# When the next weight piece is prepared, and two fill calls of one group, in a fused retention and two-MLP kernel

## Chip, cores and metric

One core of a Trainium2 chip runs the whole program. The metric is device time in microseconds (us), the median of several executions. TensorE (PE) multiplies, VectorE (DVE) and ScalarE (ACT) work element by element, GpSimd (POOL) helps at the start, SyncE's queue (SP) starts most DMAs. Each engine runs its own queue in the order in which the program issued it, so an instruction that waits holds up all that is behind it on that engine.

## What is computed

A retention layer (2 x 8 heads, 768 tokens, 64 channels, float32), whose output is laid out as 1536 tokens of 512 channels, and two MLPs behind it:

```python
    h = x @ w_in                                        # first MLP, 512 -> 2048
    g = np.maximum(h, 0.0) + alpha * np.minimum(h, 0.0)
    x = (g @ w_out).astype(np.float32)                  # 2048 -> 512
    h = x @ w_in2                                       # second MLP
    r = np.maximum(h, 0.0)
    return ((r * r) @ w_out2).astype(np.float32)
```

## The kernel before

**Numbers.** A float32 operand of a matmul is split into a high part (rounded, type float32r) and a low part (the rest), and each product of two operands is three matmuls: low by high, high by low, high by high. The split of an operand is a copy to the high part on ScalarE and a subtraction on VectorE.

**Stages.** The retention runs to about 53 us, the first MLP to about 309 us (its matmuls are L235 and L281; the last blocks of L281 run between those of the second MLP's first group), the second MLP to the end (L490 and L574).

**The second MLP** runs 16 groups n = 0 to 15, each one half u of the tokens (768 of them) with one pair p of the 16 slices of the hidden layer. The two halves of a group's hidden values come from seven products P0 to P6 (Strassen's scheme, six matmuls of 384 columns each, L490), into two PSUM banks px and py, with copies and sums between them. Behind them come the output matmuls of the group before, in six items of six matmuls of 512 columns (L574); group 0 has the last eight L281 items of three matmuls there. `strassen` writes the order of a group by hand:

- P0 into px, then ScalarE's copy of px to py (L515), and the split of the second half of the group before (L507, L508)
- fill 0; two output items; P1 into py, copy u2 on ScalarE (L523); P2 into px; relu and square of one quarter (ScalarE L502, VectorE L503)
- fill 1; one item; P3 into py, copy u3 on ScalarE (L531)
- fill 2; one item; P4 into a new px, VectorE's sum of px and u3 (L538)
- fill 3; P5 into py, relu and square (L502, L503), split of the first half (L507, L508); one item; P6 into px, VectorE's L547 and L550
- fill 4; one item

P1 waits for L515, P3 for L523, P5 for L531, P6 for L538, P0 of the next group for the L503 behind P5. In group 0 a last L281 item ends a sum on VectorE (L302) and writes it out on SP's queue (L308).

**The fills.** `fill(us)` takes steps from the generators in the list `fillers`, the first one first, until the costs that they yield use up its budget; a call with budget 0 takes none. Two generators stand there. `convert_pairs` turns the weights of the second MLP into high and low parts, 16 pieces k (two slices each, even k for the first matrix, odd k for the second; an even piece also gets four sums for Strassen's scheme). `split_x` prepares the seven token operands of a half; while it has steps it stands first. The steps of piece k, with their costs, are:

- shift (VectorE L372, cost 0.7), sign (VectorE L374, 1.2)
- the two low parts of piece k-1 (VectorE L360, 1.2 each for an even piece, 0.7 each for an odd one); then the buffer of k-1's bits is free
- start of piece k+1 (ScalarE L344 and L345, in the buffer that k-1 had, from the raw words of k+1) and, in the same step, the add of piece k (VectorE L381, 1.2)
- the raw words of k are free, the loads of piece k+2 go on SP's queue (L332, two of 512 KB); for an even piece two sums (L389, L390, cost 0.8), then two more (L392, L393, 0.8)
- two copies to the high part (ScalarE L399), in one step with the shift of piece k+1

The copies wait until the places of the weights in SBUF are free (pieces from 8 on reuse places of earlier pairs); till then a fill passes to nothing. `need` forces steps when a group asks for a weight that isn't there yet. The fills also run twice in each of the last 16 steps of the first MLP, with a budget of 1.2.

Of the kernel before, what the change touches and what calls it, by code (L numbers as in the profile page):

```python
# [41 lines left out]
BLOCKS = 2 * HALF // CH  # L42
GROUPS = [(0, p) for p in range(4)] + [(1, p) for p in range(NPF)] + [(0, p) for p in range(4, NPF)]
FILL = 1.2, 2.0, 1.2, 0.7, 1.5
KB = 256
ORDER = [(n // B, n % B) for n in range(NN)]

# [16 lines left out]
class Block:  # L64
# [8 lines left out]
    def free(self):  # L73
        n = self.words // KB
        self.units[self.at : self.at + n] = [True] * n


class Memory:
# [3 lines left out]
    def add(self, ap):  # L82
        self.spans.append((ap, [True] * (ap.shape[1] // KB)))

# [32 lines left out]
def retention_then_two_mlps(  # L117
# [100 lines left out]
    def release(blocks):  # L218
        for block in blocks:
            block.free()  # L220
# [102 lines left out]
    def convert_pairs():  # L323

        raw, bit, done = {}, {}, {}

        def load(k):
            if k < len(pieces):
                half, p = pieces[k]
                raw[k] = yield from taken(LOW, RAW + 8 * (k % 2), 8)  # L330
                for e in range(2):
                    nc.sync.dma_start(  # L332
                        raw[k].view(U32)[:, 2 * e * DM : 2 * (e + 1) * DM],
                        w2[2 * (2 * p + e) + half],
                    )

        def start(k):
            if k < len(pieces):
                half, p = pieces[k]
                bit[k] = yield from taken(LOW, BIT + 7 * half, 4 if half else 7)  # L340
                both = raw[k].view(U32, 2)
                low, high = both[:, :, 0], both[:, :, 1]
                x = bit[k].view(F32)[:, 0 : 2 * DM]
                nc.scalar.activation(x, high.bitcast(F32), AF.Copy, scale=REBIAS)  # L344
                nc.scalar.activation(low.bitcast(I32), low, AF.Copy, scale=2.0**-29)  # L345

        def cuts(k):
            half, p = pieces[k]
            x, b = bit[k].view(F32), done[k]
            if half:  # L350
                for e in range(2):
                    yield x[:, e * DM : (e + 1) * DM], b[e].ap, b[2 + e].ap
            else:
                for c in slice(0, 2 * DM), slice(2 * DM, None):
                    yield x[:, c], b[0].ap[:, c], b[1].ap[:, c]

        def lows(k):
            if k >= 0:
                for x, hi, lo in cuts(k):
                    nc.vector.tensor_tensor(lo, x, hi.bitcast(F32), ALU.subtract)  # L360
                    yield 0.7 if pieces[k][0] else 1.2
                bit.pop(k).free()
                pairs[pieces[k]] = done.pop(k)

        yield from load(0)
        yield from load(1)
        yield 0
        yield from start(0)
        for k, (half, p) in enumerate(pieces):
            both = raw[k].view(U32, 2)  # L370
            x = bit[k].view(U32)[:, 0 : 2 * DM]
            nc.vector.tensor_scalar(x, x, 3, None, ALU.logical_shift_left)  # L372
            yield 0.7
            nc.vector.scalar_tensor_tensor(  # L374
                x, both[:, :, 1], 0x80000000, x, ALU.bitwise_and, ALU.bitwise_or
            )
            yield 1.2
            yield from lows(k - 1)
            yield from start(k + 1)
            x = x.bitcast(I32)  # L380
            nc.vector.tensor_tensor(x, x, both[:, :, 0].bitcast(I32), ALU.add)  # L381
            yield 1.2
            raw.pop(k).free()
            yield from load(k + 2)
            if half == 0:
                a11, a12, a21, a22, s1, s2, s4 = (
                    bit[k].view(F32)[:, i * DM // 2 : (i + 1) * DM // 2] for i in range(7)
                )
                nc.vector.tensor_tensor(s1, a21, a22, ALU.add)  # L389
                nc.vector.tensor_tensor(s2, s1, a11, ALU.subtract)  # L390
                yield 0.8
                nc.vector.tensor_tensor(a21, a11, a21, ALU.subtract)  # L392
                nc.vector.tensor_tensor(s4, a12, s2, ALU.subtract)  # L393
                yield 0.8
            done[k] = []
            for span, at in PAIRS_AT[p % 4][2] if half else PAIRS_AT[p % 4][0:2]:
                done[k].append((yield from taken(span, at, 2 if half else 7)))
            for x, hi, lo in cuts(k):
                nc.scalar.copy(hi, x)  # L399
        yield from lows(len(pieces) - 1)  # L400
# [52 lines left out]
    def fill(us):  # L453
        for gen in list(fillers):
            while us > 0:
                cost = next(gen, "end")
                if cost == "end":
                    fillers.remove(gen)
                if cost is None or cost == "end":
                    break  # L460
                us -= cost

    def need(table, key, gen):
        while key not in table:
            cost = next(gen)
            assert cost is not None, (key, "no room")
        return table[key]

    makers = {}
# [8 lines left out]
    def strassen(n, items):  # L478

        u, p = GROUPS[n]  # L480
        v = sum(b <= n for b in begins) - 1
        banks = (n % 2,), (1 - n % 2,)
        def product(ps, i, start=False):
            name, a = WANTED[i]
            xh, xl = (x.view(F32R, HALF) for x in need(x_parts, (v, name), makers["x", v]))
            wh, wl = (w.view(F32R) for w in need(pairs, (0, p), makers["w"]))
            for c in range(2):
                cols = slice((2 * a + c) * 128, (2 * a + c + 1) * 128)
                for j, (w, x) in enumerate(((wl, xh), (wh, xl), (wh, xh))):
                    nc.tensor.matmul(  # L490
                        ps, w[:, cols], x[:, c, :], start=start and c == 0 and j == 0,
                        stop=c == 1 and j == 2, skip_group_check=True,
                    )
            if n in ends:
                release(x_parts.pop((v, name)))

        def other(count=1):
            for item in islice(items, count):
                item()

        def relu_square(out, ps):
            nc.scalar.activation(out, ps, AF.Relu)  # L502
            nc.vector.scalar_tensor_tensor(out, ps, 0.0, out, ALU.max, ALU.mult)  # L503

        def halves(block):
            hi, lo = borrow(F32R), borrow(F32R)
            nc.scalar.copy(hi.view(F32R), block.view(F32))  # L507
            nc.vector.tensor_tensor(lo.view(F32R), block.view(F32), hi.view(F32), ALU.subtract)  # L508
            spare[F32].append(block)
            return hi, lo  # L510

        px = bank(f"p1_{n}", banks[0])[:, 0:HALF]
        product(px, 0, True)
        py = bank(f"p6_{n}", banks[1])[:, 0:HALF]
        nc.scalar.copy(py, px)  # L515
        if n > 0:
            pending.pop()()
        fill(FILL[0])
        other(2 if n > 0 else 4)
        product(py, 1)  # L520
        us = borrow()
        u2, u3 = (us.view(F32, HALF)[:, i] for i in range(2))
        nc.scalar.copy(u2, py)  # L523
        product(px, 2)
        first_half = borrow()
        g = first_half.view(F32, HALF)
        relu_square(g[:, 0], px)
        fill(FILL[1])
        other(1 if n > 0 else 2)
        product(py, 3)  # L530
        nc.scalar.copy(u3, py)  # L531
        fill(FILL[2])
        other()
        px = bank(f"p5_{n}", banks[0])[:, 0:HALF]
        product(px, 4, True)
        second_half = borrow()
        h = second_half.view(F32, HALF)
        nc.vector.tensor_tensor(h[:, 1], px, u3, ALU.add)  # L538
        fill(FILL[3])
        product(py, 5)  # L540
        relu_square(g[:, 1], py)
        ga = halves(first_half)
        other()
        product(px, 6)
        if n == visits[p][-1]:
            release(pairs.pop((0, p)))
        nc.vector.tensor_tensor(h[:, 0], px, u2, ALU.add)  # L547
        spare[F32].append(us)
        h = second_half.view(F32)
        nc.vector.scalar_tensor_tensor(h, h, 0.0, h, ALU.max, ALU.mult)  # L550
        gs = [ga, None]

        def late():
            gs[1] = halves(second_half)

        pending.append(late)
        fill(FILL[4])
        other()
        return gs

# [436 lines left out]
```

## Time and profile before

| what | value |
|---|---|
| median of 3 runs | 579.86 us (577.70 to 580.03) |
| the profiled execution's own time | 579.38 us |
| its span, first to last instruction | 577.3 us |
| TensorE busy | 565.1 us, 98% |
| VectorE busy | 379.3 us, 66% |
| ScalarE busy | 309.6 us, 54% |
| share of TensorE in the chain that ended last | 85% |

A stretch of a timeline row is its start, its length, engine and line, and in brackets how long the engine had been idle and what ended that. The end of a matmul is modelled, so a row's start is compared with the start of a later row.

### The profile page before, as it was taken

How to read it: one execution, taken by the hardware profiler on the slowest of the kernel's cores; microseconds unless marked ns; L12 is line 12 of the kernel's file. 1: busy time of each engine (PE TensorE's matmuls, PEld its weight loads, DVE VectorE, ACT ScalarE, POOL GpSimd, SP SyncE). 2: the span in 40 equal slices, each digit the busy share in tenths (PEclk: the TensorE clock that was granted, in tenths of full speed). 3: DMA queues.
4: the chain of work that ended last, by engine and by line, in shares of the span. 5: the costliest groups of instructions: out<-in, count | busy, mean ns of one | idle time of the engine just before them, and what ended most of it. 6: DMA issues, size and time to landing. Idle time of an engine off the chain costs nothing.

```text
span 577.3 us, 8029 instructions
## 1 busy us (share of the span) xinstructions
PE 565.1 (98%) x3154; PEld 485.5 (84%) x3154; DVE 379.3 (66%) x552; ACT 309.6 (54%) x506; POOL 33.9 (6%) x34
## 2 busy tenths in 40 slices
PE   8999999999999999999999799999999999999997
PEld 8887888888888888888888599899888988898985
DVE  3897866666666667887575786656777783752235
ACT  2666775765746766666465453465455543452221
POOL 2784000000000000000000000000000000000000
PEclk9999999999999999999999989999999999999999
DMA  7992343323533252434800535012013500023002
GB/s 261 383 391 102 110 145 110 128 91 110 196 132 110 80 196 89 165 127 146 307 22 0 179 115 182 0 74 99 32 59 140 182 1 1 0 93 127 1 0 109
DMA packets 30148, 69.20 MB, mean 120 GB/s; under 512 B 3224, under 2 KB 7328, under 8 KB 30112
## 3 DMA queue, kind: packets, MB, share of 16 engines
q1 hardware_dynamic: 26512, 55.60, 26.9%
q10 hardware_dynamic: 3600, 13.11, 6.7%
q8 instruction: 24, 0.39, 0.3%
q14 instruction: 12, 0.10, 0.1%
HBM read 56.63 MB, written 12.07 MB: 119 GB/s over the span
## 4 chain that ended last, share of the span: by engine, by line
PE 85%; DVE 5%; ACT 4%; DMA 4%; issue 1%; SPq 0%; ACTq 0%; DVEq 0%
PE h L235 23%; PE acc L281 22%; PE acc L574 19%; PE p L490 16%; PE o L771 2%; PE o L779 2%; PE s L734 1%; DMA q<-in_qt_dram 1%; ACT low_mem L344 1%; ACT low_mem L345 1%; PE pk L794 1%; DMA r<-in_kr_dram 1%; DMA zd<-z 1%; DMA low_mem<-in_w_dram 1%; DVE low_r_mem L360 1%
## 5 line engine op out<-in xcount | busy, mean ns | idle before, releaser
L574 PE MATMUL acc<-high_r_mem,low_r_mem 128*128 128x512 f32 x288 | 73.4, 396 | 0.2
L574 PE MATMUL acc<-low_r_mem 128*128 128x512 f32 x288 | 73.0, 393 | 0.0
L281 PE MATMUL acc<-low_r_mem,high_r_mem 128*128 128x512 f32 x288 | 69.6, 389 | 0.0
L281 PE MATMUL acc<-low_r_mem 128*128 128x512 f32 x288 | 69.4, 389 | 0.0
L235 PE MATMUL h<-low_r_mem,high_r_mem 128*128 128x512 f32 x288 | 69.2, 389 | 0.0
L235 PE MATMUL h<-low_r_mem 128*128 128x512 f32 x288 | 69.0, 390 | 0.0
L252 DVE SCALAR_TENSOR_TENSOR high_mem<-h,high_mem 128x512 f32<-128x512 f32 x44 | 30.4, 690 | 52.4 <-ACT high_mem L251 52.3
L281 PEld LDWEIGHTS acc<-low_r_mem 128*128 128x128 f32 x288 | 54.0, 188 | 11.5 <-DVE high_mem L302 0.3
L235 PEld LDWEIGHTS h<-low_r_mem 128*128 128x128 f32 x288 | 54.0, 188 | 11.4 <-issue 0.2
L235 PEld LDWEIGHTS h<-low_r_mem,high_r_mem 128*128 128x128 f32 x288 | 54.0, 188 | 11.2
L281 PEld LDWEIGHTS acc<-low_r_mem,high_r_mem 128*128 128x128 f32 x288 | 54.0, 188 | 11.0
L574 PEld LDWEIGHTS acc<-high_r_mem,low_r_mem 128*128 128x128 f32 x288 | 54.1, 190 | 10.3 <-DVE low_r_mem L508 1.0
L574 PEld LDWEIGHTS acc<-low_r_mem 128*128 128x128 f32 x288 | 53.4, 188 | 9.0
L490 PE MATMUL p<-low_r_mem 128*128 128x384 f32 x288 | 57.0, 341 | 2.9 <-ACT p L515 2.7
L490 PEld LDWEIGHTS p<-low_r_mem 128*128 128x128 f32 x288 | 51.7, 190 | 6.7 <-ACT p L515 3.1
L257 ACT CAST low_r_mem<-high_mem 128x512 fp32r<-128x512 f32 x48 | 29.8, 621 | 51.0 <-DVE high_mem L252 37.8
L490 PE MATMUL p<-low_r_mem,high_r_mem 128*128 128x384 f32 x288 | 55.5, 336 | 0.3 <-DVE high_mem L503 0.3
L490 PEld LDWEIGHTS p<-low_r_mem,high_r_mem 128*128 128x128 f32 x288 | 51.1, 188 | 3.4 <-DVE high_mem L503 0.7
L508 DVE TENSOR_TENSOR low_r_mem<-high_mem,low_r_mem 128x768 fp32r<-128x768 f32 x32 | 30.6, 956 | 27.8 <-ACT low_r_mem L507 27.8
L262 DVE TENSOR_TENSOR low_r_mem<-high_mem,low_r_mem 128x512 fp32r<-128x512 f32 x48 | 33.2, 692 | 16.2 <-ACT low_r_mem L257 13.7
L503 DVE SCALAR_TENSOR_TENSOR high_mem<-p,high_mem 128x384 f32<-128x384 f32 x32 | 17.8, 556 | 38.7 <-ACT high_mem L502 38.7
L250 ACT ACTIVATE high_mem<-h 128x512 f32<-128x512 f32 x44 | 26.2, 596 | 31.7 <-PE h L235 31.7
(97 smaller groups left out, 726.9 us busy)
## 6 DMA issues: line engine op xcount, KB each, us to landing
low_mem<-in_w_dram SPq DMA_DIRECT2D x39, 512.0 KB, 4.1
low_mem<-in_w_dram ACTq DMA_DIRECT2D x25, 512.0 KB, 3.3
sums<-high_mem SPq DMA_DIRECT2D x22, 256.0 KB, 2.2
high_mem<-xs SPq DMA_DIRECT2D x12, 384.0 KB, 5.7
high_mem<-sums SPq DMA_DIRECT2D x16, 256.0 KB, 5.5
k<-in_kt_dram SPq DMA_DIRECT2D x12, 256.0 KB, 5.8
q<-in_qt_dram SPq DMA_DIRECT2D x12, 256.0 KB, 5.0
v<-in_vr_dram SPq DMA_DIRECT2D x12, 256.0 KB, 5.8
```

Source lines behind the costliest of these rows:

```text
L235: nc.tensor.matmul(ph, w[:, cols], x[:, c, :], start=c == 0 and i == 0, stop=c == NC - 1 and i == 2)
L250: nc.scalar.activation(g, ph, AF.Relu, scale=-1.0)
L252: nc.vector.scalar_tensor_tensor(g, ph, 0.0, g, ALU.max, ALU.subtract)
L257: nc.scalar.copy(gh.view(F32R)[:, 0:TT], g)
L262: nc.vector.tensor_tensor(gl.view(F32R)[:, 0:TT], g.view(F32)[:, 0:TT], gh.view(F32)[:, 0:TT], ALU.subtract)
L281: nc.tensor.matmul(acc[t][i], w[:, cols], g, start=f == part[0] and j == 0, stop=f == part[-1] and j == 2,)
L490: nc.tensor.matmul(ps, w[:, cols], x[:, c, :], start=start and c == 0 and j == 0, stop=c == 1 and j == 2, skip_group_check=True,)
L503: nc.vector.scalar_tensor_tensor(out, ps, 0.0, out, ALU.max, ALU.mult)
L508: nc.vector.tensor_tensor(lo.view(F32R), block.view(F32), hi.view(F32), ALU.subtract)
L574: nc.tensor.matmul(acc2[j], g[:, e, rows], w, start=n in begins and e == 0 and i == 0, stop=n in ends and e == 1 and i == 2,)
L771: nc.tensor.matmul(po[t * D : (t + 1) * D, a, :], v_t[:, 2 * a + t, :], sc[:, t, a, :], start=a == 0, stop=c == 0, skip_group_check=True,)
L779: nc.tensor.matmul(po[d, a, :], state[b, c % 2][d, a, :], q_t[d, a, :], start=False, stop=True, skip_group_check=True,)
```

## The change

In `convert_pairs` the start of piece k+1 moves from ahead of the add of piece k to behind it. The add yields 1.2, so the start now belongs to the next step: that with the loads of piece k+2 and, for an even piece, the first two sums, or, for an odd one, the copies and the next shift. The costs stay. The budgets of group 0 become `FILL_0`, with 0 in place of 1.2 and 0.7 for fills 2 and 3. `need` takes the end of a generator without an exception, as long as the weight is there by then.

```diff
 FILL = 1.2, 2.0, 1.2, 0.7, 1.5
+FILL_0 = 1.2, 2.0, 0.0, 0.0, 1.5
...
             yield 1.2
             yield from lows(k - 1)
-            yield from start(k + 1)
             x = x.bitcast(I32)
             nc.vector.tensor_tensor(x, x, both[:, :, 0].bitcast(I32), ALU.add)
             yield 1.2
+            yield from start(k + 1)
             raw.pop(k).free()
             yield from load(k + 2)
...
         while key not in table:
-            cost = next(gen)
+            cost = next(gen, "end")
             assert cost is not None, (key, "no room")
+            assert cost != "end" or key in table
...
+        budget = FILL if n > 0 else FILL_0
...
-        fill(FILL[0])
+        fill(budget[0])
...
-        fill(FILL[1])
+        fill(budget[1])
...
-        fill(FILL[2])
+        fill(budget[2])
...
-        fill(FILL[3])
+        fill(budget[3])
...
-        fill(FILL[4])
+        fill(budget[4])
```

## Rows read from the trace of the kernel before

**Rows 1.** The page: TensorE's busy time; granted clock of forty slices, in tenths.

```profile
PE 565.1 (98%) x3154; PEld 485.5 (84%) x3154; DVE 379.3 (66%) x552; ACT 309.6 (54%) x506; POOL 33.9 (6%) x34
...
PEclk9999999999999999999999989999999999999999
```

**Rows 2.** TensorE's waits: line and releaser, us in total, times, longest.

```profile
PE p L490 <- ACT p L515: 2.7, 1, 2.7
...
PE p L490 <- DVE high_mem L538: 1.4, 1, 1.4
```

**Rows 3.** Timeline of TensorE, second MLP: start, length, engine, line, count.

```profile
313.17 2.27 PE L490 MATMUL p<-low_r_mem,high_r_mem 128*128 128x384 f32 x12
...
320.51 0.86 PE L281 MATMUL acc<-low_r_mem,high_r_mem 128*128 128x512 f32 x3
...
330.92 3.28 PE L490 MATMUL p<-low_r_mem 128*128 128x384 f32 x12 [2.69 <-ACT p L515]
...
345.48 2.92 PE L574 MATMUL acc<-low_r_mem 128*128 128x512 f32 x12
...
348.24 2.27 PE L490 MATMUL p<-low_r_mem 128*128 128x384 f32 x12
...
363.88 2.27 PE L490 MATMUL p<-low_r_mem,high_r_mem 128*128 128x384 f32 x12
...
410.87 2.27 PE L490 MATMUL p<-low_r_mem 128*128 128x384 f32 x12
...
426.96 2.27 PE L490 MATMUL p<-low_r_mem,high_r_mem 128*128 128x384 f32 x12
...
443.47 2.27 PE L490 MATMUL p<-low_r_mem,high_r_mem 128*128 128x384 f32 x12
...
459.11 2.27 PE L490 MATMUL p<-low_r_mem 128*128 128x384 f32 x12
...
475.10 2.27 PE L490 MATMUL p<-low_r_mem 128*128 128x384 f32 x12
```

**Rows 4.** Timeline of VectorE and ScalarE, groups 0 and 1.

```profile
318.47 1.28 DVE L302 TENSOR_TENSOR high_mem<-acc,high_mem 128x512 f32<-128x512 f32 x2
...
318.59 1.14 ACT L399 CAST low_r_mem<-low_mem 128x512 fp32r<-128x512 f32 x2 [0.18 <-DVE low_mem L381]
...
319.67 0.68 DVE L372 TENSOR_SCALAR low_mem<-low_mem 128x1024 uint32<-128x1024 uint32 x1
...
320.38 1.23 DVE L374 SCALAR_TENSOR_TENSOR low_mem<-low_mem 128x1024 uint32<-128x1024 uint32 x1
...
322.13 0.55 DVE L538 TENSOR_TENSOR high_mem<-p,high_mem 128x384 f32<-128x384 f32 x1
...
323.77 0.84 ACT L507 CAST low_r_mem<-high_mem 128x768 fp32r<-128x768 f32 x1 [2.58 <-DVE high_mem L503]
...
328.35 1.15 ACT L344 ACTIVATE low_mem<-low_mem 128x1024 f32<-128x1024 f32 x1 [3.73 <-DVE low_r_mem L360]
...
330.38 0.49 ACT L515 COPY p<-p 128x384 f32<-128x384 f32 x1
```

**Rows 5.** Windows: stretch, us, busy PE, PEld, DVE, ACT, POOL, PEclk, DMA, GB/s.

```profile
332.10:335.50 3.40, 3.40 (x11) 3.11 (x11) 2.69 (x7) 1.75 (x3) 0.00 (x0) 0.50 0.41 157
...
330.92:348.24 17.32, 17.32 (x78) 15.62 (x79) 14.20 (x20) 9.59 (x14) 0.00 (x0) 0.90 0.45 154
...
348.24:363.88 15.64, 15.64 (x79) 14.08 (x78) 9.04 (x15) 6.69 (x10) 0.00 (x0) 1.00 0.34 127
```

**Rows 6.** Timeline of ScalarE, groups 6 and 7.

```profile
415.54 1.19 ACT L344 ACTIVATE low_mem<-low_mem 128x1024 f32<-128x1024 f32 x1 [1.87 <-DVE high_r_mem L360]
...
436.06 1.13 ACT L344 ACTIVATE low_mem<-low_mem 128x1024 f32<-128x1024 f32 x1 [2.83 <-DMA low_mem<-in_w_dram]
```

**Rows 7.** DMA issues from 300 to 350: median us from issue to landing.

```profile
low_mem<-in_w_dram SPq DMA_DIRECT2D x6, 512.0 KB, 3.9
```

**Rows 8.** Waits from 210 to 309, the end of the first MLP.

```profile
ACT high_mem L250 <- PE h L235: 12.5, 10, 2.7
```

## The prediction

> **What bounds the kernel now.** I read the busy table first: TensorE is busy 98% of the span, at the full granted clock in all but one of its forty slices [rows 1], so only the few places where it stands still can give time back, and an instruction saved on another engine is worth nothing by itself. The list of TensorE's own waits comes next. In the second MLP its two long entries are 2.7 us for ScalarE's copy at L515 and 1.4 us for VectorE's add at L538 [rows 2]; in the last sixteen steps of the first MLP, where the moved pair is issued as well, TensorE's matmuls have no entry. Then TensorE's timeline. Every group has the same work: seven products and six blocks of output. The start of P1 P2 (twelve matmuls of L490 in one row) marks its pace: 348.24 to 363.88 is 15.64 us undisturbed [rows 3]. Against that:
> - Group 0 to 1: 313.17 to 330.92, 17.75. Undisturbed it would be 7.34 (to 320.51), the last L281 block 0.69, P6 and P0 at 1.05 each and two output blocks 2.76 (345.48 to 348.24): 12.89, so P1 would start at 326.06. Lost 4.86.
> - Group 1 to 2: 330.92 to 348.24, 17.32. Lost 1.68.
> - Groups 6 to 7, 7 to 8, 9 to 10 (410.87 to 426.96, 443.47 after 426.96, 475.10 after 459.11): 16.09, 16.51, 15.99. Lost 0.45, 0.87 and 0.35.
>
> Together 8.21 us, which is all there is to win here.
>
> **Who causes them.** In group 0, P6 stands for L538, which VectorE ran at 322.13 to 322.68 behind the shift (L372), the sign step (L374) and a sum (L302) [rows 4]; it was wanted at 321.20. Then L344, the first half of the start, stood 3.73 us at the head of ScalarE's queue for the second low part (L360), and L515 behind it ran only at 330.38 [rows 4]; TensorE stood 2.69 us more. After these two stands the granted clock of the next 3.40 us is 0.50, the 1.2 GHz level, and 1.00 behind it [rows 5]: that is group 1's 1.68. In group 6 L344 stood 1.87 for L360 with L531 behind it; in group 7 it stood 2.83 for its DMA with L502 behind it [rows 6], so that P0 of group 8 began late.
>
> **The change, part by part.** I counted the budgets of each fill call through both orders (a call takes steps until its budget is used up). No cost and no number of steps changes, so up to group 0's fill 1 the calls hold the same steps and only the start goes one step back, behind the add. Pieces by number, old order:
> - group 0: fill 1 low4b, start6, add5; fill 2 copies5, shift6, sign6; fill 3 low5a; fill 4 low5b, start7, add6.
> - group 1: sums6 | copies6, shift7, sign7, low6a | low6b | start8, add7 | copies7, shift8, sign8.
> - group 2: low7a, low7b | start9, add8, half of sums8 | the other half | nothing | nothing.
>
> New order:
> - group 0: fill 1 low4b, add5; fills 2 and 3 nothing; fill 4 start6, copies5, shift6, sign6.
> - group 1: low5a, low5b | add6, start7, half of sums6 | the other half, copies6, shift7 | sign7 | low6a, low6b.
> - group 2: add7 | start8, copies7, shift8, sign8, low7a | low7b, add8 | start9, half of sums8 | the other half.
>
> From group 3 on both are at the same step, since there the fills go to the x parts. No weight is asked for before it is ready, so the rewritten `need` runs no extra step: nothing.
>
> *Fill 2 of group 0 empty.* L372 and L374, 0.68 and 1.23 us, leave VectorE's queue ahead of L538. The third L302 then starts about 319.7 (its block is done at 318.4), ends 320.4, and L538 ends 320.9, before 321.20. P6's wait of 1.5 us goes; the cover left is 0.3 us.
>
> *The start out of the wait.* In group 0 the pair now stands in fill 4 behind the add's call, and its slot was freed by low4b in fill 1: no 3.73 us. But start6 and copies5 still stand ahead of L515. P5 ends 320.5; L502 ends 321.2, L503 321.8, L507 (0.84) 322.65. L344 and L345 take 2.03 (328.35 to L515 at 330.38), the two copies about 1.1, so L515 starts near 325.7 and P1 near 326.2, against 326.06 undisturbed. Loss 0.15. Bounds: 0, if L502 comes a little sooner, and 3.2, the whole burst, if nothing covers it; I take 0.15, from the rows of these very instructions [rows 4]. Gain of group 0: 4.86 - 0.15 = 4.71. With no stand over 0.3 us the clock has no reason to fall: 1.68 more. Bounds there: 0 and 1.68; I take all of it, since the shorter stands of groups 6, 7 and 9 left the clock full [rows 1].
>
> *Groups 1 and 2 take what group 0 leaves.* VectorE is now busy 14.20 and 9.04 us in the stretches of groups 1 and 2 [rows 5]. By the durations of the steps (shift 0.68, sign 1.23, add 1.22, low parts 1.37 or 2.17 a pair, four sums 1.7) group 1 has 8.4 us of them in place of 8.9, group 2 7.4 in place of 4.3, which makes 13.7 and 12.1, both under the 15.64 that TensorE needs. The tightest places: L531 of group 1 behind start7 (which waits for low5b until 329.6) ends 332.2, wanted by P5 at 333.2; L531 of group 2 behind start8 and copies7 has 0.6 left; L538 there too. Cost 0; with the cover gone at all three, 0.5 each.
>
> *DMAs.* Load7 was issued in fill 2; it now stands in SP's queue behind the write of the last L308. That write waits for its L302, which ends at 324.2 in the new order (L508's 0.96 behind L507, then 0.6), so load7 goes at about 324.7 and lands 3.9 us later [rows 7], at 328.6 for its first half and 329.2 with the second. Start7 wants it at 329.6: cover 0.4. Load8 moves from 329.5 to 331.4, wanted at 344; the x loads no longer wait behind load9.
>
> By the Trainium skill, DMA: Bandwidth & Descriptors, section Bandwidth, a transfer of 1 MB has its DMA engines busy 6.15 us; an estimate from that page would have load7 landing at 330.9, L531 ending 333.4 and P5 0.3 late, 572.3 in all. The row of this trace (3.9 us for half a MB, two side by side) disagrees and decides.
>
> *Groups 5 to 9.* Same steps, start one call later. Group 6: L531 no longer waits behind L344 and the 0.45 goes; start11 and copies10 then push L502 to 420.1, and P0 still has 1.5 us. Group 7: start13 moves behind L502 and L507, when its DMA has landed; 0.87 goes. Group 9: start15 now lies right ahead of copies14, which waited for the sums anyway: its 0.35 stays (bounds 0 and 0.6).
>
> *The end of the first MLP.* Five starts move there by one step, 2.03 us each. ScalarE's L250 stands 12.5 us in ten waits for TensorE in that stretch [rows 8]: that is the cover. Cost 0; if it were gone, still under the two steps by which the second matmuls lag.
>
> **Sum.** 4.71 + 1.68 + 0.45 + 0.87 = 7.71. The profiled execution took 579.38 (span 577.3): 571.7. Its time lies 0.48 under the median of the runs, 579.86, by which it is 572.15. I say 572.0.
>
> **Rivals.**
> 1. *The burst ahead of L515 and load7 cost more.* If L538 or L503 slips by 1 us, P1 of group 1 slips as much; if load7 lands 1.5 us later, P5 does by 0.7. For it: covers of 0.3 and 0.4 only. Against: each number above is a row of the same instruction. 2.0 us lost: 574.0.
> 2. *The change only moves the wait.* P1 of group 1 is held by the whole burst, 3.2 in place of 0.15, the clock falls as now (1.68), and P5 is 0.3 late in two groups: 5.3 lost, 577.3, no change. For it: L515 still has four instructions ahead of it. Against: it needs ScalarE to begin the burst 3 us later than L507's end, and nothing in the new order holds it there.
> 3. *Slower.* The start becomes a wait for DMA, as the 2.83 of group 7 [rows 6], in nine calls in place of one, each ahead of a copy that feeds TensorE. Price: 2.83 + 2.03 less the 1.75 us between L531's earliest end and P5, 3.1 each; six of these stand before L531 or L515: 572 + 19 = 591. It decides from the point where a load comes less than 3.9 us ahead of its start. Against: the shortest distance in the new order is 4.9 us (load7), then 5.7 (load9).
>
> **How the numbers follow.** Forecast 0.68 (571.0 to 573.0), rival 1 0.20 (573 to 575), rival 2 0.08, rival 3 0.04. Half a per cent, 2.9 us, is about what a measurement of this kernel tells from no change: faster is under 577.0, and the forecast and rival 1 are there: 0.88; same 0.08; slower 0.04. Range: from 570.6 (all 8.21 won, and the runs' spread) to 575.0.
>
> **What would show it.** P1 P2 of group 1 at about 326.2 and of group 2 15.6 later; granted clock 1.00 from 326 on; no wait of L344 for L360; P6 of group 0 right behind the last L281; group 7 to 8 at 15.64; an idle time under 0.5 us left in group 9. I would be wrong if L515 of group 1 starts after 327, if L344 waits for its DMA in group 1, or if P5 or P6 of groups 1 and 2 show a wait for L531 or L538.

## The result and the profile after

The changed kernel takes 572.3 us (570.3 to 572.64, six runs), the kernel before 580.16 beside it (577.7 to 582.12, six runs): ratio 0.9862, 95% interval 0.9841 to 0.9883. The forecast was 572.0 and 570.6 to 575.0. In the changed kernel lines 345 to 400 are one behind those of the kernel before and those from 493 on three behind: L345 is the old L344, L493 the old L490, L506 the old L503, L510 and L511 the old L507 and L508, L518 the old L515, L534 the old L531, L541 the old L538.

The page's busy row and its row of the granted clock, as [rows 1]:

```profile
PE 563.5 (99%) x3154; PEld 486.1 (85%) x3154; DVE 379.6 (67%) x552; ACT 309.8 (54%) x506; POOL 33.0 (6%) x34
...
PEclk9999999999999999999999999999999999999999
```

All the waits of TensorE that the view lists now, in the form of [rows 2] (line, releaser, us in total, times, longest), are at the start of the program; the second MLP has left the list:

```profile
PE s L737 <- DMA q<-in_qt_dram: 1.4, 1, 1.4
PE warm_ps L656 <- POOL warm L651: 1.0, 1, 1.0
PE o L774 <- PE pk L797: 0.7, 1, 0.7
```

TensorE's timeline, the same places as [rows 3] (start, length, engine, line, count): P1 of groups 0, 1, 2 and of 6 to 10, and between the first two the last L282 item with P6 behind it.

```profile
314.10 2.27 PE L493 MATMUL p<-low_r_mem,high_r_mem 128*128 128x384 f32 x12
...
321.44 0.86 PE L282 MATMUL acc<-low_r_mem,high_r_mem 128*128 128x512 f32 x3
322.13 1.22 PE L493 MATMUL p<-high_r_mem 128*128 128x384 f32 x6
...
327.13 2.35 PE L493 MATMUL p<-low_r_mem 128*128 128x384 f32 x12
...
342.86 2.27 PE L493 MATMUL p<-low_r_mem 128*128 128x384 f32 x12
...
405.49 2.27 PE L493 MATMUL p<-low_r_mem 128*128 128x384 f32 x12
...
421.13 2.27 PE L493 MATMUL p<-low_r_mem,high_r_mem 128*128 128x384 f32 x12
...
436.77 2.27 PE L493 MATMUL p<-low_r_mem,high_r_mem 128*128 128x384 f32 x12
...
452.41 2.27 PE L493 MATMUL p<-low_r_mem 128*128 128x384 f32 x12
...
468.14 2.27 PE L493 MATMUL p<-low_r_mem 128*128 128x384 f32 x12
```

| distance from P1 to P1 | undisturbed | before | after |
|---|---|---|---|
| group 0 to 1 | 12.89 | 17.75 | 13.03 |
| group 1 to 2 | 15.64 | 17.32 | 15.73 |
| group 6 to 7 | 15.64 | 16.09 | 15.64 |
| group 7 to 8 | 15.64 | 16.51 | 15.64 |
| group 9 to 10 | 15.64 | 15.99 | 15.73 |
| lost in all | | 8.21 | 0.32 |

So 7.89 us came back in these five places. The profiled span went from 577.3 to 570.3, 7.0 us: P1 of group 0 lies 0.93 later in this execution (314.10 against 313.17). That comes from the retention, ahead of everything that the change touches; the last two pairs of runs below settle it.

A 9 in the row of the granted clock leaves room for a short fall: in this trace of the changed kernel 3.40 us of the retention stand at 0.50. Behind them the clock is full to the end of the work, the second MLP included (the view is that of [rows 5]):

```profile
12.00:15.40 3.40, 3.40 (x36) 3.06 (x34) 1.03 (x2) 0.00 (x0) 0.00 (x0) 0.50 0.99 323
```

ScalarE, VectorE and SP's queue in groups 0 and 1, as [rows 4]:

```profile
321.20 0.55 DVE L541 TENSOR_TENSOR high_mem<-p,high_mem 128x384 f32<-128x384 f32 x1
...
323.49 1.14 ACT L345 ACTIVATE low_mem<-low_mem 128x1024 f32<-128x1024 f32 x1
...
325.55 1.15 ACT L400 CAST low_r_mem<-low_mem 128x512 fp32r<-128x512 f32 x2
325.62 7.42 SPq L333 DMA_DIRECT2D low_mem<-in_w_dram  x4
...
326.58 0.50 ACT L518 COPY p<-p 128x384 f32<-128x384 f32 x1
...
330.66 1.16 ACT L345 ACTIVATE low_mem<-low_mem 128x1024 f32<-128x1024 f32 x1 [0.65 <-DVE low_r_mem L361]
```

L541 ends 0.38 ahead of P6. The first L345 has no wait, and the burst of L345, L346 and the two copies runs straight into L518, 0.05 ahead of the P1 that it releases at 327.13. The second L345 waits 0.65 for VectorE, and not for load7, whose issue opens the SP row at 325.62.

### The profile page after: what moved, and what is told of

The parts are those of the page before. It is cut to its first block, busy times and chain, and to the rows that moved or that the text cites. A ratio compares the mean times of both kernels' runs of the same rounds, so it can differ in the third digit from the quotient of the medians.

```text
span 570.3 us, 8025 instructions
## 1 busy us (share of the span) xinstructions
PE 563.5 (99%) x3154; PEld 486.1 (85%) x3154; DVE 379.6 (67%) x552; ACT 309.8 (54%) x506; POOL 33.0 (6%) x34
## 4 chain that ended last, share of the span: by engine, by line
PE 97%; DMA 1%; DVE 1%; issue 0%; SPq 0%; DVEq 0%
PE acc L577 23%; PE acc L282 23%; PE h L236 23%; PE p L493 21%; PE o L774 2%; PE s L737 2%; PE o L782 2%; PE pk L797 1%; DMA q<-in_qt_dram 1%; PE warm_ps L656 0%; DMA lam_sb<-in_lam_dram 0%; DVE err L696 0%; DVE low_mem L598 0%; DVE low L697 0%; DVE power L683 0%
## 5 line engine op out<-in xcount | busy, mean ns | idle before, releaser
L577 PE MATMUL acc<-high_r_mem,low_r_mem 128*128 128x512 f32 x288 | 72.2, 393 | 0.0
L282 PE MATMUL acc<-low_r_mem,high_r_mem 128*128 128x512 f32 x288 | 69.6, 389 | 0.0
L282 PE MATMUL acc<-low_r_mem 128*128 128x512 f32 x288 | 69.4, 390 | 0.0
L282 PEld LDWEIGHTS acc<-low_r_mem 128*128 128x128 f32 x288 | 54.0, 188 | 11.5 <-DVE high_mem L303 0.3
L282 PEld LDWEIGHTS acc<-low_r_mem,high_r_mem 128*128 128x128 f32 x288 | 54.0, 188 | 11.0
L493 PE MATMUL p<-low_r_mem 128*128 128x384 f32 x288 | 55.5, 336 | 0.0
L493 PE MATMUL p<-low_r_mem,high_r_mem 128*128 128x384 f32 x288 | 55.4, 335 | 0.0
L493 PEld LDWEIGHTS p<-low_r_mem 128*128 128x128 f32 x288 | 51.0, 188 | 3.1 <-ACT p L518 0.4
L493 PEld LDWEIGHTS p<-low_r_mem,high_r_mem 128*128 128x128 f32 x288 | 51.2, 188 | 2.8
L511 DVE TENSOR_TENSOR low_r_mem<-high_mem,low_r_mem 128x768 fp32r<-128x768 f32 x32 | 30.6, 957 | 24.1 <-ACT low_r_mem L510 24.1
L263 DVE TENSOR_TENSOR low_r_mem<-high_mem,low_r_mem 128x512 fp32r<-128x512 f32 x48 | 33.3, 693 | 16.2 <-ACT low_r_mem L258 13.7
L506 DVE SCALAR_TENSOR_TENSOR high_mem<-p,high_mem 128x384 f32<-128x384 f32 x32 | 17.8, 557 | 35.3 <-ACT high_mem L505 35.3
```

The source lines that it names most:

```text
L263: nc.vector.tensor_tensor(gl.view(F32R)[:, 0:TT], g.view(F32)[:, 0:TT], gh.view(F32)[:, 0:TT], ALU.subtract)
L282: nc.tensor.matmul(acc[t][i], w[:, cols], g, start=f == part[0] and j == 0, stop=f == part[-1] and j == 2,)
L493: nc.tensor.matmul(ps, w[:, cols], x[:, c, :], start=start and c == 0 and j == 0, stop=c == 1 and j == 2, skip_group_check=True,)
L577: nc.tensor.matmul(acc2[j], g[:, e, rows], w, start=n in begins and e == 0 and i == 0, stop=n in ends and e == 1 and i == 2,)
```

## The experiments

Theory: two head-of-line waits, each with its own cause (VectorE's steps ahead of the sum before P6; the start ahead of ScalarE's copies L515, L531 and ahead of L502), and a fall of the clock behind the stands. Main rival: one of the two edits does all the work in group 0 and the other only moves time about.

### One edit without the other

The start moved, old budgets:

```diff
-FILL_0 = 1.2, 2.0, 0.0, 0.0, 1.5
+FILL_0 = FILL
```

> The start moved as in the change, but the fills of group 0 keep their old budgets. My theory: two causes overlap in group 0. L372 and L374 stay ahead of L538, so P6 still stands 1.5 us and L508 0.36; but fill 4 holds only VectorE steps now, so L515 waits for nothing on ScalarE and the 2.8 us stand and the fall of the clock behind it go. Lost before group 1: about 2.0 us in place of 4.86, group 1 undisturbed (15.64 between P1 of groups 1 and 2), groups 6 to 9 as in the changed kernel. Gain against before about 6.0 us (ratio 0.990), 1.9 us slower than the changed kernel. Rival A (the empty calls alone clear group 0, the move helps groups 6 to 9 only): gain 1.6 us, L344 still stands over 3 us ahead of L515. Rival B (the empty calls do nothing by themselves): as the changed kernel, gain 7.9.

Measured: 573.51 us, ratio 0.9902 (0.9884 to 0.992), 5.65 us gained. TensorE's timeline of this kernel: P1 of group 0, P6, P1 of groups 1 and 2.

```profile
312.85 2.27 PE L493 MATMUL p<-low_r_mem,high_r_mem 128*128 128x384 f32 x12
...
322.41 1.31 PE L493 MATMUL p<-high_r_mem 128*128 128x384 f32 x6 [1.37 <-DVE high_mem L541]
...
327.74 2.27 PE L493 MATMUL p<-low_r_mem 128*128 128x384 f32 x12
...
343.38 2.27 PE L493 MATMUL p<-low_r_mem 128*128 128x384 f32 x12
```

14.89 and 15.64: P6's wait is still there, that for L518 is gone, and in this trace the clock stayed full behind the one stand of 1.37. Groups 6 and 7 take 15.64 and 15.65 and group 9 15.74, as in the changed kernel to 0.01. Rival A wanted 1.6 us, rival B 7.9.

The other edit alone, the start back in its old place:

```diff
             yield from lows(k - 1)
+            yield from start(k + 1)
             x = x.bitcast(I32)
...
             yield 1.2
-            yield from start(k + 1)
             raw.pop(k).free()
```

> The old place of the start, but fills 2 and 3 of group 0 empty. My theory: start6 stays in fill 1, where its wait is short, and fill 4 holds only copies5 ahead of L515, so all of group 0 and the clock in group 1 are cleared by this part alone: P1 of group 1 12.9 us behind P1 of group 0, 15.64 to group 2. Groups 6, 7 and 9 keep their 0.45, 0.87 and 0.35. Gain against before about 6.5 us (ratio 0.989), 1.4 us slower than the changed kernel. Rival B (the empty calls clear only P6, the move clears L515): gain 1.5 to 2 us.

Measured: 573.32 us, ratio 0.990 (0.9881 to 0.9919), 5.84 gained. The same places and groups 6 to 10 of its timeline:

```profile
313.75 2.27 PE L493 MATMUL p<-low_r_mem,high_r_mem 128*128 128x384 f32 x12
...
326.68 2.27 PE L493 MATMUL p<-low_r_mem 128*128 128x384 f32 x12
...
404.95 2.27 PE L493 MATMUL p<-low_r_mem 128*128 128x384 f32 x12
...
421.02 2.27 PE L493 MATMUL p<-low_r_mem,high_r_mem 128*128 128x384 f32 x12
...
433.42 1.33 PE L493 MATMUL p<-low_r_mem,high_r_mem 128*128 128x384 f32 x6 [0.41 <-DVE high_mem L506]
...
437.70 2.27 PE L493 MATMUL p<-low_r_mem,high_r_mem 128*128 128x384 f32 x12
```

Group 0 takes 12.93: the empty calls alone clear it, the wait for L518 included, because with fewer steps taken in fills 2 and 3 the start of piece 7 falls into another call. So for group 0 the main rival holds: the move adds nothing there (13.03 with both edits). Groups 6, 7 and 9 keep their loss (16.07, 16.68 and 16.03). By the distances, 6.10 of the 8.21 us come back with the move alone, 6.31 with the empty calls alone and 7.89 with both, so the two edits overlap. Either one takes away the stand at P1, and no fall of the clock follows in its trace; only the empty calls free P6, only the move frees groups 6, 7 and 9.

The times of these two kernels gain 0.5 us less than the distances say (5.65 and 5.84), and those of the next two 0.8 and 1.0 less. In five of the seven executions of the kernel before beside them, the granted clock leaves no room for its fall of 3.40 us (see The clock, below), so there was less to win; that this is the reason was not shown.

### The last groups alone

The changed kernel up to piece 8, the old place from there on:

```diff
             yield from lows(k - 1)
+            if k >= 8:
+                yield from start(k + 1)
             x = x.bitcast(I32)
...
             yield 1.2
-            yield from start(k + 1)
+            if not (k >= 8):
+                yield from start(k + 1)
```

> As the changed kernel up to piece 8, from there the start of the next piece stands ahead of the add again. My theory: group 6 has its 0.45 us back (L344 waits for L360 ahead of L531), group 7 its 0.87 (L344 waits for a DMA ahead of L502), group 9 its 0.35; all before is as in the changed kernel. 1.6 us slower than the changed kernel (ratio to before 0.989). Rival: those waits came from the time shift that group 0 gave to what follows, and group 7's DMA lands in time without it: 0 to 0.5 us slower.

Measured: 573.81 us, ratio 0.9903 (0.9887 to 0.9918). Its timeline (three lines later again: L496 is L490, L537 is L531, L509 is L503):

```profile
404.46 2.27 PE L496 MATMUL p<-low_r_mem 128*128 128x384 f32 x12
...
411.75 1.33 PE L496 MATMUL p<-low_r_mem 128*128 128x384 f32 x6 [0.15 <-ACT high_mem L537]
...
420.54 2.27 PE L496 MATMUL p<-low_r_mem,high_r_mem 128*128 128x384 f32 x12
...
432.94 1.32 PE L496 MATMUL p<-low_r_mem,high_r_mem 128*128 128x384 f32 x6 [0.41 <-DVE high_mem L509]
...
437.20 2.27 PE L496 MATMUL p<-low_r_mem,high_r_mem 128*128 128x384 f32 x12
```

16.08 in group 6 and 16.66 in group 7, with the same two releasers as before, and 16.02 in group 9. By the distances that is 1.75 us more than the changed kernel, where 1.6 was expected. The losses there belong to the start's place and not to the time at which group 0 hands over.

### One empty call

```diff
-FILL_0 = 1.2, 2.0, 0.0, 0.0, 1.5
+FILL_0 = 1.2, 2.0, 0.0, 0.7, 1.5
```

> As the changed kernel, but fill 3 of group 0 keeps its budget of 0.7. By the budgets fill 3 then takes start6, the copies of piece 5 and the shift of piece 6, ahead of the L502 behind P5; fill 4 takes the sign step and a low part. My theory: ScalarE's burst of 3.2 us delays L502 by 0.8 and the split L507, L508 by as much: the third matmul of the first output item waits about 0.6 us, and P1 of group 1 comes 13.5 us behind P1 of group 0 in place of 13.03: 0.5 us slower than the changed kernel (ratio to before 0.987). Rival: fill 3 doesn't matter, 13.03 as in the changed kernel, or L515 now comes early enough for 12.9.

Measured: 573.77 us, ratio 0.9904 (0.9888 to 0.992). P1 of group 1 comes 13.63 behind P1 of group 0 (13.5 expected), but group 1 then takes 16.57, which the theory had not. Timeline of ScalarE in group 1, and of TensorE (P1 of groups 0 and 1, P5 of group 1, P1 of group 2):

```profile
332.80 1.79 ACT L400 CAST high_r_mem<-low_mem 128x1024 fp32r<-128x1024 f32 x2 [0.54 <-DVE low_mem L393]
334.49 0.47 ACT L534 COPY high_mem<-p 128x384 f32<-128x384 f32 x1
```

```profile
313.60 2.27 PE L493 MATMUL p<-low_r_mem,high_r_mem 128*128 128x384 f32 x12
...
327.23 2.27 PE L493 MATMUL p<-low_r_mem 128*128 128x384 f32 x12
...
335.02 1.31 PE L493 MATMUL p<-low_r_mem 128*128 128x384 f32 x6 [0.66 <-ACT high_mem L534]
...
343.80 2.27 PE L493 MATMUL p<-low_r_mem 128*128 128x384 f32 x12
```

One step more in fill 3 brings later steps of the generator into earlier calls: copies6 now fall into fill 1, ahead of L534, and wait for the sums. I had worked the budgets out for group 0 alone. 1.4 us are lost by the distances.

### The burst ahead of L518, lengthened

Two more copies of L345 for piece 6 in the changed kernel (here L346; the copy before P1 is L519), then four more:

```diff
-                nc.scalar.activation(x, high.bitcast(F32), AF.Copy, scale=REBIAS)
+                for i in range(3 if k == 6 else 1):
+                    nc.scalar.activation(x, high.bitcast(F32), AF.Copy, scale=REBIAS)
```

> The changed kernel with L344 of piece 6 (ScalarE's copy of the high words) issued three times in place of once, with the same result, so two more instructions of about 1.04 us stand ahead of L515 in group 0. My theory: ScalarE's queue ahead of L515 sets P1 there with no slack left, so P1 of group 1 comes 2.1 us later (15.1 behind P1 of group 0), a stand of about 2.2 us; after one stand of that size the clock stays full, group 1 15.6 to 15.9. Rival A: there is 0.5 us or more of slack ahead of L515, P1 slips by 1.6 or less. Rival B: one stand of 2.2 us is enough for the clock to fall, group 1 over 17.

> As the one with two more, but four more instructions, about 4.15 us. My theory: P1 of group 1 comes 17.2 behind P1 of group 0, TensorE stands 4.3 us, and then the granted clock falls to 0.50 for some 3.4 us as in the kernel before: group 1 takes 17.2 to 17.4, the kernel 5.9 us longer than the changed one and so within 0.5% of the kernel before. Rival: the fall of the clock in the kernel before had nothing to do with the stands (it comes at the start of some runs too); group 1 takes 15.6 to 15.9.

One execution each: 575.72 and 580.49 us, the kernel before 579.2 beside them. Two more:

```profile
322.88 3.50 ACT L346 ACTIVATE low_mem<-low_mem 128x1024 f32<-128x1024 f32 x3
...
328.32 0.48 ACT L519 COPY p<-p 128x384 f32<-128x384 f32 x1
...
328.86 3.91 PE L494 MATMUL p<-low_r_mem 128*128 128x384 f32 x12 [2.28 <-ACT p L519]
...
346.15 2.09 PE L494 MATMUL p<-low_r_mem 128*128 128x384 f32 x11
```

The clock there, in the view of [rows 5] (PEclk is the third figure from the end):

```profile
329.20:332.60 3.40, 3.40 (x12) 3.40 (x11) 2.16 (x3) 0.85 (x2) 0.00 (x0) 0.50 0.06 22
332.60:346.15 13.55, 13.55 (x67) 12.01 (x67) 11.28 (x17) 7.26 (x10) 0.00 (x0) 1.00 0.54 194
```

And four more, TensorE and the clock:

```profile
332.33 4.21 PE L494 MATMUL p<-low_r_mem 128*128 128x384 f32 x12 [4.61 <-ACT p L519]
...
350.81 1.40 PE L494 MATMUL p<-low_r_mem 128*128 128x384 f32 x7
```

```profile
331.54:338.36 6.82, 6.03 (x17) 5.64 (x18) 3.71 (x6) 3.76 (x7) 0.00 (x0) 0.50 0.01 2
```

P1 of group 0 lies at 313.49 and 314.64, so P1 of group 1 comes 15.37 and 17.69 behind it, 2.34 and 4.66 later than in the changed kernel: one for one, with no slack, at 1.17 us for each added instruction and not the 1.04 that I had taken from the pair. On the clock my theory fell and rival B held: in this execution one stand of 2.28 us is enough, 3.40 us at 0.50 (1.2 GHz) begin 0.34 behind it, and group 1 takes 17.29, as it took 17.32 in the kernel before. With the stand of 4.61 us the clock is at 0.50 for 6.82 us, from 0.79 before the stand's end, and group 1 takes 18.48, where 17.2 to 17.4 was expected. Four instructions of ScalarE in the wrong place cost all that the change had won, in the one execution of each kernel that was taken.

### The changed kernel again, and start6 early

The changed kernel beside a version that keeps the start of piece 6 alone in its old place, in fill 1 of group 0 where its wait is short:

```diff
             yield from lows(k - 1)
+            if k == 5:
+                yield from start(k + 1)
...
-            yield from start(k + 1)
+            if not (k == 5):
+                yield from start(k + 1)
```

> The changed kernel itself, beside the parts on one chip. My theory: the same distances as in its first trace (13.03 from P1 of group 0 to P1 of group 1, 15.73 to group 2, 15.64 for groups 6, 7 and 8), ratio to before 0.986 to 0.988, and the start of the second MLP's P1 of group 0 within 1.3 us of the other traces, since the retention's first 15 us differ from run to run by about 1 us. Rival: the 0.9 us by which its first trace came to group 0 later than the kernel before is an effect of the change; then it is there again, by 0.5 us or more against every trace whose starts stand in the old place.

> The changed kernel, but the start of piece 6 alone stands in its old place, ahead of the add of piece 5 in fill 1 of group 0. My theory: the burst ahead of L515 shrinks to the two copies, so P1 of group 1 comes 12.93 us behind P1 of group 0 in place of 13.03, and group 1 is 15.64 in place of 15.73: 0.2 us faster than the changed kernel in the trace, which its timing can't tell (ratio to the changed kernel 0.9995 to 1.0). Rival: start6 in fill 1 delays L531 or L538 in group 0 as it delays L531 in group 6: 13.4 or more.

Measured: 572.4 us, ratio 0.9887 (0.9859 to 0.9916, where 0.986 to 0.988 was expected), and 571.07 us, ratio 0.987 (0.9847 to 0.9894). In the changed kernel P1 of groups 0, 1 and 2 starts at 314.22, 327.26 and 343.01; the rows of the version with start6 early (L496 is L490):

```profile
313.55 2.27 PE L496 MATMUL p<-low_r_mem,high_r_mem 128*128 128x384 f32 x12
...
326.48 2.27 PE L496 MATMUL p<-low_r_mem 128*128 128x384 f32 x12
...
342.12 2.27 PE L496 MATMUL p<-low_r_mem 128*128 128x384 f32 x12
```

13.04 and 15.75 against 12.93 and 15.64: 0.22 us, as expected. The medians lie 1.3 us apart, so both were timed again.

> The changed kernel, timed more closely beside the version with start6 early on one chip. My theory: the two differ by the 0.2 us that the traces show in groups 0 and 1; the 1.3 us between their medians in three rounds came from the retention, whose end lay at 54.35 in the one trace and 53.72 in the other. With five rounds the medians lie within 0.8 us of each other. Rival: the version with start6 early is 1 us or more faster again.

> The version with start6 in its old place, five rounds. My theory: median within 0.8 us under the changed kernel's, P1 of group 0 some 259.9 us behind the first matmul of the first MLP as in all traces, 12.93 and 15.64 for groups 0 and 1. Rival: 1 us or more under the changed kernel's median, with the first MLP beginning earlier in most executions.

Measured: 571.47 us (ratio 0.9868, 0.9843 to 0.9893) and 571.83 us (ratio 0.986, 0.9839 to 0.988). The 1.3 us did not come again; the distances did (13.01 and 15.73; 12.96 and 15.64). The version with start6 early saves 0.1 to 0.2 us in the traces and nothing that its timing shows.

Where the scatter is: the first matmul of the first MLP begins at 53.33 in the kernel before, at 54.22, 54.35 and 53.93 in the three traces of the changed kernel, and between 52.98 and 54.77 in the others. P1 of group 0 follows it 259.8 to 259.9 us later in all twelve. So the 0.93 us of the first trace is scatter of the retention, and the five starts moved in the first MLP cost nothing. What makes the retention scatter was not tried. TensorE's waits there for the load of q differ from trace to trace (0.3 to 1.5 us in all), and the 3.40 us at 0.50 in the first trace can't be all of it: the second trace of the changed kernel has no such stretch and reaches the first MLP still later.

## Why the prediction was right

**What bounds.** The stands of TensorE, with the clock behind one of them, were what there was to win: 7.89 of the 8.21 us in [rows 3] came back, and the time fell by 7.9 us. That the two agree so closely is luck: beside the kernel before, the changed kernel gained 7.9, 6.8 and 8.5 us in its three timings (580.16 to 572.3, 579.2 to 572.4, 579.98 to 571.47).

**Order of the steps.** The budgets counted through gave the order that the trace shows: L541 behind the third sum, start6, the copies and then L518 in fill 4, load7 behind the write of the last sum.

**Group 0.** P6 needed L538 by 321.20 and was to have it at 320.9; in the trace L541 ends at 321.75 and P6 starts at 322.13, the same 0.3 to 0.4 us of cover. P1 was to come 13.03 to 13.04 behind P1 (326.2 against 313.17) and came 13.03 behind. The burst was taken from the same four instructions in [rows 4]. It costs 0.10 (13.03 against the 12.93 of the version with start6 early), and the longer bursts show that nothing more hides behind it: each further instruction moved P1 by its whole length. What the prediction did not see is that the empty calls alone take away the wait for L515 too; it gave that gain to the move.

**The clock.** The 1.68 us of [rows 5] went as forecast, 1.59 of it net. The reason given was incomplete: I spoke of two stands, and in one execution a single one of 2.28 us was enough, while in another 1.37 us left the clock full. And the 1.68 is the price in the traced execution, not in every one. Of the 25 other timed executions of the kernel before whose clock is on record, 10 have a mean granted clock of 0.999 or 1.000; one stretch of 3.40 us at 0.50 would make it 0.997. Their spans are 576.3 us in the mean, those of the other 15, with 0.994 to 0.997, 577.5. So the fall behind the stands seems not to come each time, though the waits in these executions were not traced. What decides it was not tried, and the prediction took the whole term as if it always came.

**Groups 1 and 2.** They took what group 0 left without a wait of TensorE for L534 or L541. VectorE was busy 14.60 and 11.98 us in their stretches, where 13.7 and 12.1 was worked out. Load7 went out at 325.62, which is 324.7 on the scale of the kernel before, as worked out. L345 stood 0.65 for VectorE and not for this load, which must therefore have landed by 330.66. An estimate from the 6.15 us that the Trainium skill (DMA: Bandwidth & Descriptors, section Bandwidth) gives for 1 MB issued from GpSimd would have it there at 331.8; this load, two transfers of 512 KB issued from SP, was there earlier. The 3.9 us that the forecast took for it is the median of six transfers that run from 3.3 to 5.3 us in the kernel before, so the cover of 0.4 was less sure than it looked. The 0.09 that group 1 still loses is in its row of P1 and P2, 2.35 us long in place of 2.27.

**Groups 6 and 7.** 0.45 and 0.87 came back as forecast, and the kernel with the old place there lost 0.44 and 1.02 again.

**Group 9, the term that was off.** I had the 0.35 stay, since the copies waited for the sums anyway. They waited less: in the kernel before, the start in fill 0 also held up L523 and L502, so that the sums came later. L502 began 2.75 behind P1 there and 2.30 in the changed kernel, the copies 5.00 and 4.76. ScalarE in group 9, the kernel before (P1 at 459.11) and the changed kernel (P1 at 452.41):

```profile
459.43 1.16 ACT L344 ACTIVATE low_mem<-low_mem 128x1024 f32<-128x1024 f32 x1 [1.67 <-issue]
...
461.86 0.50 ACT L502 ACTIVATE high_mem<-p 128x384 f32<-128x384 f32 x1
464.11 1.79 ACT L399 CAST high_r_mem<-low_mem 128x1024 fp32r<-128x1024 f32 x2 [1.75 <-DVE low_mem L392]
```

```profile
454.71 0.49 ACT L505 ACTIVATE high_mem<-p 128x384 f32<-128x384 f32 x1 [0.50 <-PE p L493]
...
457.17 1.77 ACT L400 CAST high_r_mem<-low_mem 128x1024 fp32r<-128x1024 f32 x2
```

0.26 of the 0.35 came back, and with the old place there 16.02 was back. The step that failed is the one that moved the start and left the rest of the group where it had been.

**Sum.** 7.71 forecast, 7.89 by the distances. Rival 1 (the covers of 0.3 and 0.4 us give way) and rival 2 (the burst holds P1) did not happen. But the longer bursts show rival 2's mechanism at work (2.34 and 4.66 us on P1, and the clock behind it), and the one with fill 3 kept shows how little the order of the steps allows: one step more in one call costs 1.4 us.

## What to carry to other kernels

Where one engine is busy nearly all the time, list its own waits and follow each to the instruction at the head of the queue that holds the releaser up; the cure is to move that one instruction behind the step that frees its buffer, or, as the empty calls did in group 0, to issue fewer steps ahead of the releaser, not to make anything faster. Count a budgeted filler through to the point where both orders meet again: a change of one call shifts later ones too. A stand of TensorE can have a second price, the clock behind it: in the traced execution a wait of 2.7 us was worth 4.4. What a part saves is read from distances inside a trace, since the retention alone scatters by 1.8 us here.

## What the runs showed of the hardware

- One stand of TensorE of 2.28 us, in dense work, was followed by 3.40 us at a granted clock of 0.50; stands of 1.37 us and less in the second MLP were not; with one of 4.61 us came 6.82 us at 0.50, 0.79 of them within the stand. Each is one execution. In 10 of 25 other executions of the kernel before the mean granted clock leaves no room for such a fall, though the one that was traced has a stand of 2.69 us and the fall.
- ScalarE's L345 (128x1024, float32) starts 1.01 to 1.09 us ahead of the L346 behind it (192 pairs in twelve traces), but 1.15 to 1.18 ahead of another L345 that writes the same buffer again (six pairs, in the two runs with a longer burst).
